# One order string, rewritten: the opening and the key, value and query stage of a transformer block

## The chip, the cores and the metric

The kernel runs on 1 core of one Trainium2 chip. The metric is device time in microseconds (us). The profile gives, beside it, a trace of one execution with the busy time of each engine: TensorE (PE, and PEld for its weight loads), VectorE (DVE), ScalarE (ACT), GpSimd (POOL) and SyncE (SP), which here issues nearly all DMAs.

## The reference

```python
# x: 2048 rows of 576, bf16; 32 heads of 18; DFF = 4608; c: one row of 576
mod = silu(c) @ w_mod                        # six rows: sa, ca, ga, sb, cb, gb
h = layernorm(x) * (1 + ca) + sa
q, k, v = split(h @ wqkv)                    # per head
pq, pk = q @ w_phi, k @ w_phi                # per head, 18 x 18
phi(p) = concat(softmax(p), softmax(-p))     # per head, 36 features
kv, z = phi(pk)^T @ v, sum_rows(phi(pk))
o = (phi(pq) @ kv) / (phi(pq) . z + 1e-6)
x = x + ga * (o @ wo)
h = layernorm(x) * (1 + cb) + sb
x = x + gb * (relu(h @ w1) @ w2)
```

## The kernel before, in words

The 2048 rows are 16 tiles of 128. Up to 90 us the kernel makes keys, values and queries for all tiles; from there on it works through the two-layer network in pairs of tiles, by loops that the change does not touch.

The first stage is a list of jobs. The string `ORDER` names them one by one, and a loop calls each (a number after a colon is the pair of PSUM banks that the job writes; pair 0 is banks 0 and 1, and so on to pair 3). Nothing is reordered afterwards: the instructions of every engine stand in its own queue in the order of the string, and an engine waits at an instruction until its data and its buffer are there. Two jobs of different engines, neither of which uses what the other writes, can therefore swap places in the string without changing any queue.

```python
    ctx.enter_context(tc.manual_schedule())
    for word in ORDER.split():
    ...
        if s:
            at[f, n] = pair(int(s))
        JOBS[f](*(() if n is None else (n,)))
```

The jobs that this document names:

- `L...` are loads by SyncE (`Lbdw` alone by ScalarE): `LwkT`, `LwqT`, `Lwv` the key, query and value weights, `Lwsc` and `Lwsh` the parts of w_mod for the scale (1 + ca) and the shift, `Lwsb` and `Lwcb` those for the second norm, `Lx...` rows of x, `Lt0` to `Lt4` blocks of x turned (features on the partitions). `wl0` to `wl4`, `w2a...` and `w2b...` load the weights of the network, `wl...` into one large buffer R1 whose start holds the early weights.
- `Z11` and `Z1` are 11 and 1 matmuls of 512 columns over zeros into bank 6, whose result nobody reads (line 238). `sc` and `sh` hold five such matmuls each, one before every five products.
- `FK` folds w_phi into the key weights: 25 small matmuls (line 450) from `LwkT` and `Lbdw`. `frd`, `fra`, `frr` copy its chunks out on VectorE and ScalarE. `FQ0` to `FQ4` (line 267) do the same for the query weights from `LwqT`, copied out by `FQrd` and `FQra`.
- `sx` (ScalarE) and `sd` (VectorE, lines 551 to 553) form silu(c). `sc` multiplies it with the scale weights on TensorE (line 259), `ca` reads the result (VectorE, line 556), `sh` does the same for the shift into the same bank, and `shc` reads that (VectorE, line 671). `m2` (line 259) and `m2c` do it for the second norm.
- `bn` are statistics of a tile on VectorE (lines 243 and 244), `sa` and `sp` the small steps on ScalarE and GpSimd that make the rows which `T` turns (TensorE, line 635) and `Tc` copies (line 638). `xd`, `xp`, `xa` multiply two tiles of turned x by the scale, on VectorE, GpSimd or ScalarE (lines 572, 565, 570).
- `KR` and `VR` (line 276) make the rows for mean and shift of the key and value weights, brought back by `KRh`, `KRd`, `VRh`, `VRd`. `QR` is the same for queries.
- `K`, `V`, `Q` are projections of a tile, 10 matmuls of 288 columns (line 282); `Ka` and `Kb` are the first 8 and the last 2 of a K. `eK` and `eQ` are their exponentials, two instructions of ScalarE (line 287); `sK` the sums on VectorE (line 292), `rK` the reciprocal by two ScalarE instructions (lines 309 and 310), `pA` and `pM` steps on GpSimd, `vE` the scaling of V on VectorE (line 313), `kv` the product of features and values (line 331).
- `sq` and `qi` send query features out and back, `qs`, `qp` and `qt` sum, scale and turn them (`qt` is a DMA that transposes, line 360). `ga`, `gb` with `gac`, `gaw`, `gar` make the two gate rows, `wo` scales the output weights by one of them. `kz`, `nu`, `ot`, `oc`, `W`, `ht` finish the first two tiles.

Of the kernel before, what the change touches and what calls it, by code (L numbers as in the profile page):

```python
# [42 lines left out]


ORDER = """
Lbdw Z11 LwkT FK Z1 fra1 Lx0 Lcc sx bn0 sd frd2 Lwsc frd0 bn1 sa0 frr sc ca Lwsh frd4 Lx2 Lid bn3 sh fra3 sp0 T0:1 shc
Lt0 KR:2 KRh0 Lwv Lx4 xd0 bn2 KRh1 mk KRd0 KRd1 Tc0 sa2 Ka0:0 VR:1 bn4 VRh0 Kb0 VRd0 sp2 VRh1 Lt1 xd2 Ka1:2 Kb1 VRd1
T2:1 eKa0 sK0 LwqT FQ3:3 Tc2 K2:0 FQra3 bn5 Lwsb eKa1 sK1 K3:3 rK0 eK2 sa4 FQ4:2 FQrd4 pM0 V0:1 sK2 Lwcb rK1 pA1 pA0
Lt2 pM1 V1:0 m2:2 eK3 FQ0:3 Lx6 vE0 V2:1 Lwga vE1 rK2 Lx10 m2c FQrd0 pA2 FQ1:3 xa4 sp4 Lt4 bn7 vE2 T4:2 Tc4 K4:0 FQra1
eK4 FQ2:2 xp6 bn6 sa6 FQrd2 sK3 Lt3 bn11 K5:1 pM2 kv0 kv1 QR:2 eK5 V3:0 kv2 QRh sp6 QRe QRd T6:2 rK3 sK4 pA3 vE3 rp  # L50
Tc6 pM3 K7:1 rK4 K6:2 pM4 pA4 eK7 eK6 Lwgb ga:0 gac V4:1 bn9 kv3 sK5 rK5 bn8 pA5 w2b0 sa8 V5:2 vE4 bn12 sp8 T8:0 xa8
pM5 vE5 Tc8 Q0:1 eQ0 gb:2 xp14 kv4 kv5 sK6 bn10 Q1:0 gbc sa10 sK7 gaw gar wl1 rK6 K8:1 qs0 wl3 bn15 eQ1 eK8 K9:2 eK9
sp10 xp10 Lwo Q2:0 pA6 sK8 pM6 eQ2 V6:1 rK8 bn13 vE6 sK9 bn14 qp0 rK7 Q3:2 pA8 T10:0 Tc10 pA7 eQ3 qs1 pM7 kv6 K10:1
eK10 rK9 K11:0 sK10 pM8 V8:2 eK11 sa14 sa12 V7:1 vE8 pM9 rK10 V9:0 vE7 xa12 sp12 pA9 kv7 T12:2 sK11 rK11 kv8 V10:1 vE9
kv9 wl0 pA10 vE10 Tc12 pM10 K12:0 sp14 T14:2 Tc14 gbw eK12 kv10 K13:1 eK13 wo2 K14:2 eK14 qt0 qs2 sK12 sK13 Q4:0 eQ4
rK13 K15:1 w2a1 qp1 V11:2 V12:0 gbr qs3 wo1 pA11 qp2 pM11 vE11 kv11 w2a2 rK12 w2a0 pA12 eK15 vE12 sK15 pM12 qt1 V13:2
kv12 pM13 Lmask sK14 Q5:1 wl4 rK15 eQ5 sq5 Q6:0 pA13 pA15 vE13 sq4 kv13 qt2 V15:2 rK14 vE15 pM15 pA14 V14:1 vE14 eQ6
Q11:2 pM14 qp3 sq6 kv14 kv15 qt3 eQ11 sq11 Q7:1 kz nu1:2 Q8:0 nu0:3 nO1 td2 eQ7 eQ8 sq7 nO0 td0 sq8 ot1:2 td1 Q9:1 oc1
Q10:0 ot0:2 wo0 wo4 eQ9 qi5 wo3 sq9 oc0 eQ10 W1:3 xr1 qi4 W0:1 lb1 Q12:2 xr0 lb0 Q13:0 lr1 eQ12 sq10 qi6 lr0 ap1 eQ13
Q14:1 ht1:2 Q15:3 ap0 wl2 ht0:0 ha eQ14 eQ15 hd w2b1 sq13 sq15 sq14 sq12  # L60
"""

SEVEN = """
# [1238 lines left out]
```

## Time and profile before

| | |
|---|---|
| median of 3 runs | 374.23 us (374.04 to 374.76) |
| the profiled execution | 374.21 us, of which the span of the trace is 372.4 us |
| TensorE busy in the span | 365.9 us (98%) |
| VectorE, ScalarE, GpSimd busy | 291.5 us (78%), 225.3 us (60%), 147.3 us (40%) |
| DMA | 50.26 MB, mean 135 GB/s |

Times in the trace count from the start of the span. Where a row ends in brackets, they hold the idle time of the engine before it and what ended it. The ends of matmuls are modelled, so the pace of TensorE is read from starts.

### The profile page before, as it was taken

To read this page: it belongs to the slowest core of one execution; us is meant where nothing else is said; L and a number is where in the kernel's file an instruction comes from. 1 tells how busy PE (TensorE), PEld (TensorE's weight loads), DVE (VectorE), ACT (ScalarE), POOL (GpSimd) and SP (SyncE) were. 2 spreads that over 40 slices of the span, in tenths; PEclk is the share of its full clock that TensorE was granted. 3 is DMA by queue.
4 is the path that set the end of the run, shared out by engine and by line. 5 is a ranking of instruction groups with operands and counts; after the bars stand their busy time and mean duration, and the time that the engine had idled before them with its cause. 6 is when DMAs were issued, how large, how long until landed. Compare 5 with 4: busy or idle time off the path is not lost.

```text
span 372.4 us, 14350 instructions
## 1 busy us (share of the span) xinstructions
PE 365.9 (98%) x6236; PEld 312.4 (84%) x6237; DVE 291.5 (78%) x540; ACT 225.3 (60%) x507; POOL 147.3 (40%) x215
## 2 busy tenths in 40 slices
PE   7999999999999999999999999999999999999996
PEld 3778788888888788889988987998799889879975
DVE  3999997679979789987897689679777857755742
ACT  2598998588632535608853874578277628835720
POOL 2167999940302567380056007402720260043023
PEclk9999999999999999999999999999999999999999
DMA  8994799787976437572164248413422304101001
GB/s 298 414 371 158 273 409 327 205 235 297 277 170 133 121 83 160 150 136 60 36 113 116 35 35 128 102 38 69 99 63 20 84 18 53 36 0 35 4 2 33
DMA packets 58880, 50.26 MB, mean 135 GB/s; under 512 B 46912, under 2 KB 51136, under 8 KB 58048
## 3 DMA queue, kind: packets, MB, share of 16 engines
q1 hardware_dynamic: 58672, 49.18, 48.9%
q8 instruction: 49, 0.80, 0.9%
q10 hardware_dynamic: 144, 0.16, 0.2%
q14 instruction: 15, 0.12, 0.1%
HBM read 32.27 MB, written 5.90 MB: 103 GB/s over the span
## 4 chain that ended last, share of the span: by engine, by line
PE 93%; DMA 4%; ACT 1%; SPq 0%; issue 0%; DVE 0%
PE PS L890 33%; PE PS L810 23%; PE PS L282 15%; PE PS L744 10%; PE PS L793 3%; DMA R<-in_wqT_dram 3%; PE PS L984 2%; PE PS L401 2%; DMA R<-in_wsc_dram 2%; PE PS L958 2%; PE PS L331 2%; PE PS L418 1%; PE PS L930 1%; ACT R L570 1%; PE PS L989 0%; PE PS L373 0%
## 5 line engine op out<-in xcount | busy, mean ns | idle before, releaser
L890 PEld LDWEIGHTS <-RH 128*128 128x128 f16 x846 | 81.5, 98 | 21.0 <-issue 0.4
L878 POOL TENSOR_TENSOR yt<-yt,gb_row 128x288 f32<-128x288 f32 x23 | 27.3, 1186 | 169.8 <-DVE yt L877 169.8
L810 PEld LDWEIGHTS <-R 64*128 64x128 bf16 (+1 forms) x1824 | 76.1, 94 | 0.7 <-issue 0.2
L890 PE MATMUL PS<-R,RH 128*128 128x288 bf16 (+1 forms) x558 | 74.5, 286 | 0.0
L810 PE MATMUL PS<-h,R 64*128 64x128 bf16 x1056 | 69.3, 216 | 0.0
L840 ACT ACTIVATE RH<-PS 128x512 f16<-128x512 f32 x96 | 50.9, 604 | 9.2 <-PE PS L810 9.1
L810 PE MATMUL PS<-RE,R 64*128 64x128 f16 x768 | 48.2, 216 | 0.0
L287 ACT ACTIVATE RT<-PS,rs 128x576 bf16<-128x576 f32 x64 | 42.9, 746 | 3.6 <-PE PS L282 3.4
L890 PE MATMUL PS<-RT,RH 128*128 128x288 f16 x288 | 38.6, 286 | 0.0
L744 PE MATMUL PS<-h,R 64*128 64x256 bf16 (+1 forms) x684 | 36.3, 264 | 0.0
L744 PEld LDWEIGHTS <-R 64*128 64x128 bf16 x684 | 31.6, 94 | 4.0 <-issue 0.2
L1047 ACT ACTIVATE h<-h,mod 128x256 bf16<-128x256 bf16 x63 | 32.8, 588 | 2.3 <-DMA h<-xn 2.3
L282 PE MATMUL PS<-RH,R 116*128 116x288 bf16 x240 | 32.5, 286 | 0.1
L810 PE MATMUL PS<-h,early 64*128 64x128 bf16 x384 | 32.0, 216 | 0.0
L282 PE MATMUL PS<-RH,RT 116*128 116x288 bf16 x240 | 31.5, 286 | 0.0
L243 DVE BATCH_NORM_STATS2 st<-x_sb 128x6 f32<-128x288 bf16 x64 | 25.8, 446 | 6.4 <-DMA x_sb<-in_xk_dram 6.3
L282 PEld LDWEIGHTS <-RT 116*128 116x128 bf16 x240 | 22.9, 98 | 5.5
L282 PEld LDWEIGHTS <-R 116*128 116x128 bf16 x240 | 22.6, 98 | 5.9 <-ACT R L638 0.4
L877 DVE TENSOR_TENSOR yt<-PS,RS 128x288 f32<-128x288 f32 x23 | 10.4, 452 | 20.6 <-PE PS L890 14.1
L810 PEld LDWEIGHTS <-w 64*128 64x128 f16 (+1 forms) x480 | 26.5, 94 | 0.0
L879 POOL TENSOR_TENSOR x_sb<-yt,x_sb 128x288 bf16<-128x288 f32 x30 | 24.9, 832 | 2.6 <-DVE yt L875 0.8
L810 PE MATMUL PS<-RE,w 64*128 64x128 f16 x384 | 25.9, 216 | 0.0
(179 smaller groups left out, 744.0 us busy)
## 6 DMA issues: line engine op xcount, KB each, us to landing
R<-in_w_dram SPq DMA_DIRECT2D x4, 1152.0 KB
eqd<-RT SPq DMA_DIRECT2D x12, 288.0 KB, 4.1
RT<-eqd SPq DMA_DIRECT2D x12, 288.0 KB, 3.0
R<-in_w2b_dram SPq DMA_DIRECT2D x2, 1296.0 KB, 6.9
R<-in_w2a_dram SPq DMA_DIRECT2D x3, 864.0 KB
out_dram<-x_sb SPq DMA_DIRECT2D x15, 144.0 KB, 1.8
x_sb<-in_xk_dram SPq DMA_DIRECT2D x10, 144.0 KB
RT<-in_xT_dram SPq DMA_DIRECT2D x2, 640.0 KB, 6.3
```

What stands on the lines that cost most here:

```text
L243: dve.bn_stats(out=s[:, hf, :], in_=x_sb[:, t % 6 if n else t, hf * HD:(hf + 1) * HD])
L282: pe.matmul(pr[:, k, 0:HD], lhsT=xt(t, ck), rhs=w[0:R, ck, k * HD:(k + 1) * HD], start=(ck == 0), stop=(ck == NC - 1))
L287: act.activation(out=E.rearrange("p (b h s e) -> p b h s e", b=2, s=2, e=DH)[:, :, :, s, :], in_=pr[:, :, 0:HD].rearrange("p b (h e) -> p ...
L744: pe.matmul(PS[:, 2 * u + hf, n * 256 + o:n * 256 + o + w], lhsT=w1_lhs(hf, c, j, h), rhs=hb[b0:b0 + 64, c, o:o + w], start=(n == 0 and c ...
L793: pe.matmul(PS[:, bank_at[n], j * 256:j * 256 + 256], lhsT=w1_lhs(hi, c, j, hi), rhs=hb[64 * hi:64 * hi + 64, c, :], start=(j == 0 and c = ...
L810: pe.matmul(PS[:, bank_at[BK[n] + str(g)], i * P:(i + 1) * P], lhsT=w[r, (4 * c + i) * P:(4 * c + i + 1) * P], rhs=x, start=(n in ("M1", " ...
L840: act.activation(out=o, in_=v[{"k11": "Y", "k12": "Z", "k21": "X", "k22": "W"}[n]], func=ACT.Relu)
L877: dve.tensor_tensor(out=y, in0=PS[:, bank, 0:HD], in1=SS[:, s, :], op=ALU.add)
L878: pool.tensor_tensor(out=y, in0=y, in1=gb_row[:, c], op=ALU.mult)
L879: eng.tensor_tensor(out=xs(t)[:, c], in0=y, in1=xs(t)[:, c], op=ALU.add)
L890: pe.matmul(PS[:, bank, 0:HD], lhsT=am[:, j, :], rhs=bm[:, j, :], start=first and j == 0, stop=(j % 9 == 8), skip_group_check=True)
L1047: act.activation(out=o, in_=o, func=ACT.Identity, scale=mod(1, c), bias=mod(0, c))
```

## The change

Only the string `ORDER` is rewritten: the same 377 jobs, in another order, some with another pair of banks. No job is added, dropped or changed.

```diff
@@ -43,21 +43,21 @@
-Lbdw Z11 LwkT FK Z1 fra1 Lx0 Lcc sx bn0 sd frd2 Lwsc frd0 bn1 sa0 frr sc ca Lwsh frd4 Lx2 Lid bn3 sh fra3 sp0 T0:1 shc
-Lt0 KR:2 KRh0 Lwv Lx4 xd0 bn2 KRh1 mk KRd0 KRd1 Tc0 sa2 Ka0:0 VR:1 bn4 VRh0 Kb0 VRd0 sp2 VRh1 Lt1 xd2 Ka1:2 Kb1 VRd1
-T2:1 eKa0 sK0 LwqT FQ3:3 Tc2 K2:0 FQra3 bn5 Lwsb eKa1 sK1 K3:3 rK0 eK2 sa4 FQ4:2 FQrd4 pM0 V0:1 sK2 Lwcb rK1 pA1 pA0
-Lt2 pM1 V1:0 m2:2 eK3 FQ0:3 Lx6 vE0 V2:1 Lwga vE1 rK2 Lx10 m2c FQrd0 pA2 FQ1:3 xa4 sp4 Lt4 bn7 vE2 T4:2 Tc4 K4:0 FQra1
-eK4 FQ2:2 xp6 bn6 sa6 FQrd2 sK3 Lt3 bn11 K5:1 pM2 kv0 kv1 QR:2 eK5 V3:0 kv2 QRh sp6 QRe QRd T6:2 rK3 sK4 pA3 vE3 rp
-Tc6 pM3 K7:1 rK4 K6:2 pM4 pA4 eK7 eK6 Lwgb ga:0 gac V4:1 bn9 kv3 sK5 rK5 bn8 pA5 w2b0 sa8 V5:2 vE4 bn12 sp8 T8:0 xa8
-pM5 vE5 Tc8 Q0:1 eQ0 gb:2 xp14 kv4 kv5 sK6 bn10 Q1:0 gbc sa10 sK7 gaw gar wl1 rK6 K8:1 qs0 wl3 bn15 eQ1 eK8 K9:2 eK9
-sp10 xp10 Lwo Q2:0 pA6 sK8 pM6 eQ2 V6:1 rK8 bn13 vE6 sK9 bn14 qp0 rK7 Q3:2 pA8 T10:0 Tc10 pA7 eQ3 qs1 pM7 kv6 K10:1
-eK10 rK9 K11:0 sK10 pM8 V8:2 eK11 sa14 sa12 V7:1 vE8 pM9 rK10 V9:0 vE7 xa12 sp12 pA9 kv7 T12:2 sK11 rK11 kv8 V10:1 vE9
-kv9 wl0 pA10 vE10 Tc12 pM10 K12:0 sp14 T14:2 Tc14 gbw eK12 kv10 K13:1 eK13 wo2 K14:2 eK14 qt0 qs2 sK12 sK13 Q4:0 eQ4
-rK13 K15:1 w2a1 qp1 V11:2 V12:0 gbr qs3 wo1 pA11 qp2 pM11 vE11 kv11 w2a2 rK12 w2a0 pA12 eK15 vE12 sK15 pM12 qt1 V13:2
-kv12 pM13 Lmask sK14 Q5:1 wl4 rK15 eQ5 sq5 Q6:0 pA13 pA15 vE13 sq4 kv13 qt2 V15:2 rK14 vE15 pM15 pA14 V14:1 vE14 eQ6
-Q11:2 pM14 qp3 sq6 kv14 kv15 qt3 eQ11 sq11 Q7:1 kz nu1:2 Q8:0 nu0:3 nO1 td2 eQ7 eQ8 sq7 nO0 td0 sq8 ot1:2 td1 Q9:1 oc1
-Q10:0 ot0:2 wo0 wo4 eQ9 qi5 wo3 sq9 oc0 eQ10 W1:3 xr1 qi4 W0:1 lb1 Q12:2 xr0 lb0 Q13:0 lr1 eQ12 sq10 qi6 lr0 ap1 eQ13
-Q14:1 ht1:2 Q15:3 ap0 wl2 ht0:0 ha eQ14 eQ15 hd w2b1 sq13 sq15 sq14 sq12
+Lbdw LwkT FK fra1 Lx0 bn0 Lcc Lwsc Lwsh Lx2 Lid Lt0 Lwv Lx4 Lt1 LwqT frd0 bn1 sx sd sa0 mk Z11 sc frd2 sp0 frd4 ca sh
+T0:0 frr bn3 Lwsb shc xd0 bn2 Z1 fra3 KR:3 Lwcb Tc0 KRh0 KRh1 KRd0 rp Lt2 Lx6 VR:2 Ka0:0 KRd1 Lt3 Kb0 sa2 xd2 VRh1
+Ka1:1 Kb1 sp2 VRh0 VRd0 T2:3 VRd1 eKa0 Lwga Tc2 eKa1 bn4 sK0 FQ3:2 FQra3 Lx10 rK0 K2:0 eK2 bn5 K3:3 pA0 eK3 FQ4:2 V0:1
+sK1 FQrd4 sK2 pM0 rK1 vE0 V1:0 pA1 vE1 sa4 rK2 m2:2 sp4 FQ0:3 pA2 FQrd0 V2:1 m2c FQ1:2 T4:3 bn6 Lt4 xa4 Tc4 K4:0 FQ2:3
+FQra1 bn7 sa6 vE2 pM2 K5:2 FQrd2 eK4 pM1 QR:1 QRh sK3 sp6 sK4 kv0 kv1 kv2 QRe QRd eK5 V3:0 xp6 sK5 T6:2 rK3 pA3 vE3
+Tc6 rK4 bn9 pM3 K7:1 pA4 rK5 K6:2 pM5 bn8 pA5 bn12 ga:0 eK7 sK7 eK6 pM4 V4:1 Lwgb gac V5:2 Q0:0 vE4 kv3 wl2 wl0 sa8
+xa8 sp8 xp14 xp10 T8:1 eQ0 kv4 vE5 kv5 Q1:2 sK6 Tc8 rK7 bn11 eQ1 gb:0 K8:1 rK6 gbc gaw bn10 bn14 K9:2 w2a0 eK8 pA6
+sa10 sK8 eK9 Q2:0 eQ2 bn15 rK8 V6:1 vE6 Q3:2 sp10 T10:0 pM7 Tc10 K10:1 Lwo pM6 qs1 bn13 eQ3 sK9 pM8 kv6 eK10 sK10
+K11:0 gar wo0 V8:2 pA8 eK11 gbw V7:1 rK9 pA7 vE7 V9:0 qp1 V10:1 vE8 pA9 sa12 sp12 vE9 sa14 sK11 T12:0 wl4 rK10 Lmask
+pA10 xa12 sp14 Tc12 K12:2 vE10 T14:0 Tc14 qs0 kv7 pM9 pM10 kv8 kv9 eK12 sK12 K13:1 rK11 qp0 qs2 eK13 rK12 sK13 w2a1
+pM11 K14:2 pM12 qt1 eK14 Q4:0 K15:1 kv10 eQ4 V11:2 gbr eK15 V12:0 w2b0 pA11 vE11 qp2 sK15 rK13 qt0 pA12 rK15 vE12 Q5:1
+wl3 pA13 sK14 pA15 Q6:2 qs3 pM13 eQ5 rK14 kv11 pA14 kv12 eQ6 pM15 sq4 V15:1 vE15 pM14 sq5 w2a2 V13:0 sq6 qp3 V14:1
+vE13 wo1 vE14 kv13 Q11:0 eQ11 kv14 kv15 Q7:2 qt2 qt3 eQ7 kz nu1:1 sq11 Q8:3 wo2 eQ8 nu0:0 nO1 w2b1 ot1:2 td2 Q9:1 oc1
+sq7 Q10:3 sq8 wo3 nO0 td1 ot0:0 eQ9 wo4 oc0 td0 W1:2 xr1 qi5 W0:1 eQ10 lb1 sq9 lr1 Q12:2 xr0 eQ12 Q13:0 sq10 lb0 lr0
+Q14:3 eQ13 qi4 ap1 ht1:2 wl1 sq12 Q15:1 ap0 ht0:0 sq13 ha hd eQ14 sq14 qi6 eQ15 sq15
```

Sorted by engine, the two strings begin so:

- TensorE before: `Z11 FK Z1 sc sh T0 KR Ka0 VR Kb0 Ka1 Kb1 T2 FQ3 K2 K3 FQ4 V0 V1 m2 FQ0 V2 FQ1 T4 K4`; after: `FK Z11 sc sh T0 Z1 KR VR Ka0 Kb0 Ka1 Kb1 T2 FQ3 K2 K3 FQ4 V0 V1 m2 FQ0 V2 FQ1 T4 K4`.
- VectorE before: `bn0 sd frd2 frd0 bn1 frr ca frd4 bn3 shc xd0 bn2`; after: `bn0 frd0 bn1 sd frd2 frd4 ca frr bn3 shc xd0 bn2`.
- SyncE, both: `LwkT Lx0 Lcc Lwsc Lwsh Lx2 Lid Lt0 Lwv Lx4 Lt1 LwqT Lwsb Lwcb Lt2 Lx6`; then before `Lwga Lx10 m2c Lt4 Lt3 QRd Lwgb`, after `Lt3 Lwga Lx10 m2c Lt4 QRd Lwgb`.

## The prediction

> **What bounds the kernel now.** I first cut the span into stretches and asked each for the busy time of the engines (columns: stretch and length, then busy time and instructions of PE, PEld, DVE, ACT, POOL, then granted clock, DMA share, GB/s).
>
> ```profile
> 1.29:5.59 4.30, 4.29 (x11) 1.41 (x11) 0.00 (x0) 0.71 (x1) 1.13 (x4) 1.00 0.87 282
> 5.59:7.13 1.54, 1.42 (x27) 1.43 (x27) 0.81 (x2) 0.64 (x2) 0.00 (x0) 1.00 1.05 428
> 12.41:17.91 5.50, 5.22 (x43) 4.53 (x43) 5.30 (x19) 3.86 (x10) 0.62 (x3) 1.00 1.02 413
> 17.91:27.92 10.01, 9.88 (x135) 8.03 (x135) 9.85 (x17) 9.49 (x28) 6.18 (x13) 1.00 0.95 375
> 27.92:90.21 62.29, 62.29 (x695) 50.90 (x697) 53.94 (x89) 52.49 (x123) 46.30 (x87) 1.00 0.80 265
> 90.21:372.40 282.19, 278.66 (x5270) 243.68 (x5270) 216.64 (x398) 156.41 (x341) 91.53 (x99) 1.00 0.39 84
> ```
>
> From 27.92 to 90.21 TensorE has work in all of 62.29 us, and from 12.41 to 27.92 it misses 0.28 and 0.13. What it does there is the same after the change, in another order. So no order can win more than these 0.4 us behind 12.41, and TensorE passes a late start at 12.41 on to the end almost whole. Only what lies ahead of 12.41 can move the time much. That is where the timeline comes in, and there the job that changes its place is `Z11`, eleven matmuls whose result nobody reads: first in TensorE's queue before, now behind `FK` and ahead of `sc`.
>
> ```profile
> 1.30 4.38 PE L238 MATMUL PS<-early 128*128 128x512 bf16 x11 [1.30 <-POOL eps_t L230]
> 2.55 0.15 PEld L238 LDWEIGHTS <-early 128*128 128x128 bf16 x1 [0.28 <-issue]
> 2.98 0.15 PEld L238 LDWEIGHTS <-early 128*128 128x128 bf16 x1 [0.28 <-issue]
> 4.69 0.15 PEld L238 LDWEIGHTS <-early 128*128 128x128 bf16 x1 [0.28 <-issue]
> 5.09 0.10 PEld L238 LDWEIGHTS <-early 128*128 128x128 bf16 x1 [0.25 <-issue]
> 5.59 1.54 PEld L450 LDWEIGHTS <-R 126*128 126x128 bf16 x25 [0.41 <-DMA R<-in_wkT_dram]
> 5.80 1.49 PE L450 MATMUL PS<-RS,R 126*128 126x126 bf16 x25
> 7.13 0.60 PE L238 MATMUL PS<-early 128*128 128x512 bf16 x2
> 8.20 0.28 PE L259 MATMUL PS<-siluc,R 116*128 116x1 bf16 x5 [0.48 <-DMA R<-in_wsc_dram]
> 12.01 0.27 PE L635 MATMUL PS<-ident,early 128*128 128x128 bf16 x2
> 12.42 1.43 PE L276 MATMUL PS<-RH,RS 116*100 116x288 bf16 x10
> 17.91 0.45 PE L267 MATMUL PS<-RS,R 126*128 126x126 bf16 x6 [0.28 <-DMA R<-in_wqT_dram]
> ```
>
> The reader is to see three things. `Z11` now runs while TensorE waits for the key weights anyway (they let `FK` go at 5.59): it costs nothing. `FK` is done when `Z1` starts at 7.13, and `sc` starts at 8.20, set by the landing of its weights. And the starts of the weight loads show the pace: 0.43 us for 512 columns from 2.55 to 4.69, then faster. In the chain of waits a group of 20 matmuls of 288 columns takes 2.45 us, which is 0.425 ns a column or 0.218 us for 512:
>
> ```profile
> 18.35 2.45 PE PS L282 x20
> ```
>
> So the first matmuls ran at half pace, until about 5.05, or 3.75 us after the first. The granted clock reads 1.00 in that stretch too; I go by the starts. That the pace comes with a while of work, rather than at a fixed time, is my reading; this trace has one start only.
>
> **The change part by part.** *`Z11` behind `FK`.* Nothing is ahead of `FK` now, so it starts at the same 5.80 (its load is first on SyncE in both orders), but at half pace. At full pace its 25 matmuls took 7.13 - 5.80 = 1.33 us; times 0.43 / 0.218 = 1.97 that is 2.6, so it ends at 8.4. Then come the eleven. If the half pace lasts 3.75 us from 5.80 as it did from 1.30, it ends at 9.55: until then 1.15 / 0.43 = 2.7 matmuls, and the other 8.3 at 0.218 take 1.8. `sc` can start at 11.35 instead of 8.20: 3.15 us late.
>
> [...]
>
> The bounds from rows: at full pace throughout, `FK` ends at 7.13 and the eleven at 7.13 + 11 x 0.218 = 9.53. Then silu(c) is later, since `sd` is moved behind `frd0` and `bn1` on VectorE:
>
> ```profile
> 6.32 0.82 DVE L243 BATCH_NORM_STATS2 st<-x_sb 128x6 f32<-128x288 bf16 x2 [6.32 <-DMA x_sb<-in_xk_dram]
> 7.17 0.21 DVE L244 BATCH_NORM_AGGREGATE mv<-st 128x2 f32<-128x12 f32 x1
> 7.30 0.12 DVE L551 TENSOR_SCALAR sg<-sg 116x5 f32<-116x5 f32 x1
> 7.67 0.17 DVE L553 TENSOR_TENSOR siluc<-ccol,sg 116x5 bf16<-116x5 bf16 x1
> 7.75 1.26 DVE L459 CAST RH<-PS 116x504 bf16<-116x504 f32 x2
> ```
>
> The statistics end at 7.38, one copy takes 0.63, the second statistics 1.06, the three silu steps 0.54: 9.6. That is the earliest start of `sc`, 1.4 us late, and at 11.35 it hides behind the eleven. At half pace throughout, `sc` starts at 8.4 + 11 x 0.43 = 13.1, 4.9 us late. I take 3.15, since the one start in this trace lasted 3.75 us.
>
> *From `sc` to `KR`.* The steps are the same, with the same waits (`sh` for `ca`, `KR` for `shc`): 12.42 - 8.20 = 4.2 us. `Z1` now stands between `T0` and `KR`, in a gap from about 12.12 (two transposes of 128 columns at 0.425 ns from 12.01) to 12.42; its 0.22 fit, and cost 0.2 if that cover went. VectorE has `frr` and `bn3`, about 1.5 us, ahead of `shc`, but `shc` waits for `sh`, about 1.8 us behind `ca`. So `KR` starts about 15.55.
>
> *The loads.* SyncE's queue has the same first sixteen loads in the same order, and nothing that it is moved past makes it wait. So, whatever the words of the change say, shift, value and query weights and the first turned blocks come no earlier than before: cost and gain nothing. Only `Lt3` goes four places up.
>
> *From `KR` to 27.92.* The query weights let `FQ3` go at 17.91 after a wait of 0.28 that the late start covers. Against that VectorE and ScalarE were busy for 9.85 and 9.49 of 10.01 us, with the same work behind `KR` in both orders, so they give TensorE little room: `FQ3` now writes the banks of `VR` and has to wait for `VRd1`. I count a gain of 0.15, between 0 and 0.4.
>
> *From 27.92 to 90.21.* No wait can go, so a new order can only add some. Two places look tight, both where `rK` is moved up on ScalarE (`rK5` ahead of `eK7`, `rK7` ahead of `eQ1`):
>
> ```profile
> 34.04 2.64 ACT L287 ACTIVATE RT<-PS,rs 128x576 bf16<-128x576 f32 x4
> 36.72 0.28 ACT L309 ACTIVATE early<-early 128x64 f32<-128x64 f32 x1
> 37.03 0.26 ACT L310 ACTIVATE early<-early 128x64 f32<-128x64 f32 x1
> 35.56 1.40 PE L282 MATMUL PS<-RH,R 116*128 116x288 bf16 x10
> 42.76 5.15 ACT L287 ACTIVATE RT<-PS,rs 128x576 bf16<-128x576 f32 x8
> ```
>
> `eK7`, the first half of the four at 34.04, ended about 35.36, and `V4` overwrites its banks from 35.56: 0.2 us of slack. The reciprocal takes 0.57 (36.72 to the next start at 37.29), so `V4` would wait about 0.35. Queued behind `rK5` are `eK7` and `eK6`. `rK7` pushes a block of eight exponentials, back to back in 5.15 us, by the same 0.57; part of it reaches `Q3`, which waits for `eK9` to leave its banks. I take 0.4 for both, between 0 (the slack is elsewhere) and 1.1 (both whole).
>
> *Near 75 us* `w2a2` (864 KB) now goes out just ahead of the transposes `qt2` and `qt3`, whose landing lets `eQ8` and `eQ9` write.
>
> ```profile
> 71.97 1.31 SPq L360 DMA_TRANSPOSE RE<-RT  x1
> DMA to landing us min/median/max: 3.6/6.7/9.7
> 78.49 1.38 ACT L287 ACTIVATE RT<-PS,rs 128x576 bf16<-128x576 f32 x2 [0.23 <-PE PS L282]
> 79.76 0.70 ACT L695 ACTIVATE oT<-PS 128x640 bf16<-128x640 bf16 x1
> 81.68 2.61 PE L418 MATMUL PS<-wo_sb,oT 128*128 128x288 bf16 x20
> ```
>
> Issued at 71.97 and landing after the median 6.7 it would come at 78.7 against `eQ8` at 78.49; behind it `oc1` ended 80.46, and `W1` began at 81.68. So 1.2 us are covered: nothing. At the longest landing, 9.7, `eQ8` would wait until 81.7, and 2.0 us would show. The late loads (`wl1` last instead of `wl2`, `w2b1` earlier) meet no wait, since nothing between 90 and 360 shows TensorE idle; nothing.
>
> *Sum*, against the profiled execution's own 374.21 (the median of the runs is 374.23, the span 372.4): 3.15 - 0.15 + 0.4 = 3.4, so 377.6.
>
> **The rivals.** *Full pace from the start.* The early half pace belongs to the first microseconds of a program, not to idleness. Then silu(c) sets `sc`: 1.4 - 0.15 + 0.4 = 1.65, so 375.9. For it: the granted clock of 1.00. Against it: that reads 1.00 where the starts show half.
>
> *Half pace through all eleven.* The half pace lasts longer this time than in the one start that I have: 4.9 - 0.15 + 0.4 = 5.15, so 379.4. For it: if what ends it is work done, `FK` starts it with shorter matmuls than the eleven were; and the runs of before can't show how much its length varies, since there a late change of pace is covered by the wait to 8.20. Against it: 3.75 us is the only length seen.
>
> *The late start is absorbed.* The loads, not TensorE, set the pace up to 17.91 (`FQ3` waits for query weights), so a late `KR` is made up. It decides if the start slips by less than that wait and the 0.13 behind it, 0.4 in all; then the rest is covered and the time is 374.2, not slower. It needs `sc` by 8.6. Against it: even at full pace the eleven end at 9.53.
>
> **How the numbers follow.** The forecast of 377.6 has 0.70, full pace 0.08, half pace throughout 0.12, absorbed 0.04; 0.06 is for something that I don't see, half of it on either side. The forecast's own range is 376.8 to 378.8: a half pace of 3.4 to 5 us, and waits behind `KR` between -0.4 and 1.1. The range from 376.2 to 379.8 adds the half pace throughout and part of what lies between; the case of full pace and the absorbed one stay outside. 0.2% is 0.75 us, about what the runs of this kernel can tell from no change. Slower by more: forecast, both paces and half of the unseen, 0.93. Within: the absorbed one, 0.04. Faster: the other half of the unseen, 0.03.
>
> **What would show it.** In the timeline after: TensorE empty until 5.8; `FK` taking about 2.6 us; weight loads of line 238 first 0.43 and then 0.22 apart; the first matmul of line 259 at 11 to 12 with no wait for a DMA; line 276 at 15 to 16; no wait of line 267 for the query weights; and at 90.2 + 3.4 = 93.6 the first line 744. The forecast is wrong if `FK` keeps its 1.33 us, if line 276 starts before 14 or after 17, or if the start of line 744 is shifted by 1 us more or less than line 276.

## The result and the profile after

The changed kernel took 378.49 us (median, 378.08 to 378.65) against 374.44 us (374.04 to 374.76) for the kernel before on the same chip: a ratio of 1.0107, 95% interval 1.0089 to 1.0125. The profiled execution took 378.65 us with a span of 376.9; the one before, 374.21 and 372.4. So the two traces differ by 4.5 us, and that is what has to be found.

First the same kind of cut as before, at the changed kernel's own marks (same columns: busy time and instructions of PE, PEld, DVE, ACT, POOL, granted clock, DMA share, GB/s).

```profile
1.29:5.59 4.30, 0.10 (x2) 0.21 (x3) 0.00 (x0) 0.71 (x1) 1.14 (x4) 1.00 0.85 285
5.49:11.06 5.57, 5.57 (x37) 3.69 (x37) 4.08 (x12) 1.76 (x6) 0.00 (x1) 1.00 1.01 389
14.87:19.93 5.06, 5.06 (x44) 4.54 (x44) 4.90 (x18) 3.41 (x10) 0.62 (x3) 1.00 1.01 416
30.00:93.91 63.91, 63.09 (x692) 50.77 (x694) 54.75 (x89) 52.85 (x122) 47.43 (x84) 1.00 0.87 265
93.91:376.70 282.79, 278.79 (x5272) 243.76 (x5270) 216.73 (x398) 156.67 (x341) 91.53 (x99) 1.00 0.36 80
```

TensorE is empty up to 5.49, then shows hardly a gap until 19.93. New is the row from 30.00 to 93.91: TensorE misses 0.82 us there, where it missed nothing in the stage before. The timeline of the changed kernel gives the marks (the second column is the length of a group; a row ends in the idle time before it and what ended that):

```profile
5.49 2.56 PE L450 MATMUL PS<-RS,R 126*128 126x126 bf16 x25 [5.49 <-DMA RS<-in_bdw_dram]
7.85 3.37 PE L238 MATMUL PS<-early 128*128 128x512 bf16 x12
8.27 0.15 PEld L238 LDWEIGHTS <-early 128*128 128x128 bf16 x1 [0.28 <-issue]
8.69 0.15 PEld L238 LDWEIGHTS <-early 128*128 128x128 bf16 x1 [0.27 <-issue]
9.12 1.61 PEld L238 LDWEIGHTS <-early 128*128 128x128 bf16 x8 [0.28 <-issue]
11.06 0.27 PE L259 MATMUL PS<-siluc,R 116*128 116x1 bf16 x5
12.74 0.16 DVE L556 TENSOR_SCALAR ca<-PS 116x5 f32<-116x5 f32 x1 [2.43 <-PE PS L259]
14.87 2.65 PE L276 MATMUL PS<-RH,RS 116*100 116x288 bf16 x20
19.93 0.44 PE L267 MATMUL PS<-RS,R 126*128 126x126 bf16 x6
86.67 1.40 PE L418 MATMUL PS<-wo_sb,oT 128*128 128x288 bf16 x10 [0.28 <-ACT oT L695]
93.91 2.29 PE L744 MATMUL PS<-h,R 64*128 64x128 bf16 x73
96.66 2.13 PE L744 MATMUL PS<-h,R 64*128 64x256 bf16 x35 [0.46 <-DMA R<-in_w_dram]
```

`FK` runs at half pace: from its start to the first of the eleven it takes 2.36 us (5.49 to 7.85) instead of 1.33. Weight loads of line 238 start 0.42 and 0.43 apart until 9.12, then eight within 1.61 us, 0.2 each: the half pace ends there. Beside the marks of before, one of which is not shown yet:

```profile
10.50 0.26 PE L259 MATMUL PS<-siluc,R 116*128 116x1 bf16 x5 [0.41 <-DVE ca L556]
90.14 4.15 PE L744 MATMUL PS<-h,R 64*128 64x128 bf16 x108
```

| first start of | before | after | later by | forecast |
|---|---|---|---|---|
| `FK` (line 450) | 5.80 | 5.49 | -0.31 | 0 |
| `sc` (line 259) | 8.20 | 11.06 | 2.86 | 3.15 |
| `KR` (line 276) | 12.42 | 14.87 | 2.45 | 3.15 |
| `FQ3` (line 267) | 17.91 | 19.93 | 2.02 | |
| line 744 | 90.14 | 93.91 | 3.77 | 3.4 |
| end of the span | 372.4 | 376.9 | 4.5 | 3.4 |

Up to `FQ3` the change costs 2.0 us. From `FQ3` to line 744 it costs another 1.75 (73.98 against 72.23) and behind line 744 another 0.73. The waits of TensorE in the changed kernel explain only part of this:

```profile
PE PS L450 <- DMA RS<-in_bdw_dram: 5.5, 1, 5.5
PE PS L744 <- DMA R<-in_w_dram: 0.5, 1, 0.5
PE PS L635 <- DVE RT L313: 0.3, 1, 0.3
PE PS L418 <- ACT oT L695: 0.3, 1, 0.3
```

A matmul group is longer in the timeline than its share of the chain: 10 of line 282 show 1.40 us in the prediction's timeline, where their share in its chain is 1.23. A gap of up to 0.17 us can therefore show as busy there, and many small ones can add up unseen. The chain of the changed kernel says what they wait for. Before, it was TensorE from 27.92 to 90.21; now it leaves TensorE in that stretch, for GpSimd and above all for four transfers:

```profile
39.30 7.77 DMA gatd<-gt
47.14 7.06 DMA ga_row<-gatd
78.31 6.23 DMA RE<-RT
88.77 7.84 DMA R<-in_w_dram
```

And the queues of SyncE, GpSimd and ScalarE at those places:

```profile
72.82 0.43 SPq L606 DMA_DIRECT2D R<-in_w2a_dram  x1
74.86 6.11 SPq L360 DMA_TRANSPOSE RE<-RT  x2
88.77 0.46 SPq L614 DMA_DIRECT2D R<-in_w_dram  x1
54.34 1.28 POOL L690 TENSOR_TENSOR wo_sb<-wo_sb,ga_row 128x576 bf16<-128x576 bf16 x1 [1.30 <-DMA ga_row<-gatd]
56.33 1.42 DVE L313 TENSOR_TENSOR RT<-PS,early 128x576 bf16<-128x576 f32 x2 [0.82 <-POOL early L652]
82.07 1.38 ACT L287 ACTIVATE RT<-PS,rs 128x576 bf16<-128x576 f32 x2 [0.70 <-DMA RE<-RT]
84.64 1.38 ACT L287 ACTIVATE RT<-PS,rs 128x576 bf16<-128x576 f32 x2 [0.61 <-DMA RE<-RT]
```

Three places, each a job that the string moved. **`wo0`** stands ahead of `pA8` and `pA7` now: GpSimd waits 1.30 us in it for the gate row, `pA` comes late, VectorE's scaling of V waits 0.82 (the row at 56.33) and then 0.38 for GpSimd, and TensorE 0.33 for VectorE (line 635 in its waits). **`w2a2`** goes out at 72.82, ahead of `qt2` and `qt3`. Their row of 6.11 us holds 3.05 and 2.66 us for the two and 0.40 between them, in which the second waited for its data from GpSimd; before, the two took 1.31 and 1.29. `eQ8` and `eQ9` wait 0.70 and 0.61 for them. **`wl1`** goes out last, at 88.77, and line 744 waits 0.46 for it at 96.66.

### The profile page after: what moved, and what is told of

Same layout as the page of the kernel before. It is cut to its first block, busy times and chain, and to the rows that moved or that the text cites. A ratio compares the mean times of both kernels' runs of the same rounds, so it can differ in the third digit from the quotient of the medians.

```text
span 376.9 us, 14356 instructions
## 1 busy us (share of the span) xinstructions
PE 366.3 (97%) x6237; PEld 313.3 (83%) x6237; DVE 292.3 (78%) x540; ACT 225.7 (60%) x507; POOL 148.1 (39%) x215
## 4 chain that ended last, share of the span: by engine, by line
PE 83%; DMA 9%; POOL 4%; ACT 2%; issue 1%; DVE 1%; SPq 0%; ACTq 0%; DVEq 0%; POOLq 0%
PE PS L890 32%; PE PS L810 23%; PE PS L744 9%; PE PS L282 5%; PE PS L793 3%; DMA R<-in_w_dram 2%; DMA gatd<-gt 2%; DMA ga_row<-gatd 2%; POOL RT L299 2%; PE PS L984 2%; DMA RE<-RT 2%; PE PS L958 2%; PE PS L238 1%; PE PS L401 1%; DMA RS<-in_bdw_dram 1%; ACT RT L287 1%
```

## The experiments

In the diffs `-` and `+` are moves in the order string. "276 to 744" is the time from the first line 276 to the first line 744 in the profile, "744 to end" from there to the end of the span; they show a delay behind the opening whatever the opening did. Each is read from one execution: the changed kernel itself took 79.04 and 80.15 us from 276 to 744 in its two. Ratios are to the kernel before on the same chip, with 95% intervals.

| kernel | first 276 | 276 to 744 | 744 to end | median us | ratio |
|---|---|---|---|---|---|
| before | 12.42 | 77.72 | 282.26 | 374.44 | |
| changed | 14.87 | 79.04 | 282.99 | 378.49 | 1.0107 (1.0089 to 1.0125) |
| changed, again | 15.79 | 80.15 | 282.26 | 378.84 | 1.0122 (1.0099 to 1.0146) |
| changed, `Z11` first | 14.14 | 80.30 | 282.66 | 377.36 | 1.0071 (1.0045 to 1.0097) |
| before, `Z11` behind `FK` | 16.42 | 77.72 | 282.16 | 377.88 | 1.0083 (1.0069 to 1.0096) |
| changed, no `Z11` | 13.00 | 78.62 | 283.78 | 377.56 | 1.0081 (1.0055 to 1.0106) |
| before, no `Z11` | 13.46 | 77.72 | 282.12 | 374.95 | 1.0007 (0.9998 to 1.0016) |
| changed, `wl1` early | 15.57 | 78.45 | 282.18 | 377.67 | 1.0088 (1.0064 to 1.0111) |
| changed, `w2a2` early | 15.11 | 78.11 | 283.28 | 379.36 | 1.0136 (1.0111 to 1.0160) |
| changed, `wo0` late | 16.18 | 78.56 | 283.96 | 379.40 | 1.0131 (1.0110 to 1.0151) |
| changed, all three moves | 16.06 | 78.55 | 282.19 | 378.05 | 1.0091 (1.0069 to 1.0113) |
| changed, opening back | 13.15 | 79.04 | 282.01 | 376.57 | 1.0063 (1.0040 to 1.0085) |
| opening and three places back | 13.02 | 77.81 | 282.47 | 374.53 | 1.0011 (0.9998 to 1.0024) |
| the same, `ca` first | 12.41 | 78.27 | 282.52 | 374.64 | 1.0002 (0.9989 to 1.0015) |

**The place of the eleven matmuls.** In the kernel before, `Z11` alone is put behind `FK`:

```diff
-Lbdw Z11 LwkT FK Z1 fra1
+Lbdw LwkT FK Z11 Z1 fra1
```

> The kernel before with Z11 alone moved behind FK. Theory: FK at half pace to about 7.9, the eleven to 10.9, Z1 to 11.1, sc 2.9 us late, less 0.4 for the wait for query weights that goes: 376.9 us, with no wait on a DMA behind 20 us. Rival (absorbed): 374.4. Rival (the opening is the whole change): 378.5.

It cost 0.83% by itself: 377.88 us, where 376.9 was expected. Its timeline:

```profile
8.10 4.67 PE L238 MATMUL PS<-early 128*128 128x512 bf16 x13
11.08 0.15 PEld L238 LDWEIGHTS <-early 128*128 128x128 bf16 x1 [0.28 <-issue]
11.51 0.77 PEld L238 LDWEIGHTS <-early 128*128 128x128 bf16 x4 [0.28 <-issue]
12.61 0.27 PE L259 MATMUL PS<-siluc,R 116*128 116x1 bf16 x5
16.42 1.43 PE L276 MATMUL PS<-RH,RS 116*100 116x288 bf16 x10
```

`FK` takes the same 2.36 us (5.74 to 8.10), but the half pace lasted to about 11.5 in this execution, 5.8 us, which the expectation did not have, and line 276 starts 4.0 late. From there to line 744 it takes 77.72 us, exactly as before, and so does the rest to 0.1: the delay of the opening is passed on whole, and nothing is added. So the forecast's main mechanism is shown on its own, and what the changed kernel loses behind the opening comes from other moves.

The other way round, in the changed kernel `Z11` alone goes back to the head:

```diff
-Lbdw LwkT FK ... sa0 mk Z11 sc frd2
+Lbdw Z11 LwkT FK ... sa0 mk sc frd2
```

> The changed kernel with Z11 alone moved back to the head of TensorE's queue. Theory (the change costs 2.0 to 2.5 us at the opening, where Z11 stands in the way of sc, and another 2 us later, where three loads come late): sc then waits for silu(c), ready at 9.13 in the changed kernel, so it starts at about 9.25 instead of 11.06, KR moves from 14.87 to about 13.1 and everything behind it by the same 1.8: about 376.7 us, with the three later waits still there. Rival (all of the loss comes from the opening, the later waits only follow from it): 374.4 us, no later waits. Rival (the opening's loss is absorbed by the loads anyway): 378.5.

It took 377.36 us, where 376.7 was expected. By the medians it got back only about a third of the loss, and its interval overlaps that of the changed kernel. The profile is of an execution of 378.86 us, 1.5 above the median. In it `sc` now waits for silu(c), the second part of the changed opening, as the forecast's rival of full pace had it (it put `sc` at 9.6, the trace says 9.30):

```profile
9.30 0.26 PE L259 MATMUL PS<-siluc,R 116*128 116x1 bf16 x5 [1.89 <-DVE siluc L553]
```

Yet line 276 starts at 14.14, 4.84 us behind `sc` instead of 4.22. Cut into microseconds, the granted clock of this execution shows why (the last but two column):

```profile
10.00:11.00 1.00, 0.92 (x18) 0.66 (x18) 0.45 (x2) 0.00 (x0) 0.00 (x0) 1.00 1.08 403
11.00:12.00 1.00, 0.98 (x13) 0.51 (x12) 0.89 (x4) 0.00 (x0) 0.91 (x5) 0.68 1.04 429
12.00:13.00 1.00, 1.00 (x14) 0.47 (x12) 0.79 (x3) 0.00 (x0) 0.07 (x1) 0.50 0.96 392
14.00:15.00 1.00, 1.00 (x6) 0.91 (x6) 1.00 (x6) 0.05 (x1) 0.00 (x0) 0.61 1.09 448
15.00:16.00 1.00, 1.00 (x10) 1.00 (x9) 0.93 (x4) 0.79 (x3) 0.09 (x1) 1.00 0.97 406
```

After the gap of 1.89 us the clock fell back to a half from about 11.4 to 14.8 (by the means of these slices). That is in this one trace; in all the others the granted clock is 1.00 from 8 to 16 us.

**Without the eleven.** Both kernels, `Z11` taken out (its result is read by nobody):

```diff
-... sa0 mk Z11 sc frd2          (changed)
+... sa0 mk sc frd2
-Lbdw Z11 LwkT FK Z1             (before)
+Lbdw LwkT FK Z1
```

> The changed kernel with Z11 left out (eleven matmuls whose result nobody reads). Theory: Z11 costs only its own length there; FK at half pace ends at 7.85, sc starts with silu(c) at 9.25 and the pace is full by about 9.2, so the time is that of e1, 376.7 (up to 377.0). Rival (the eleven are needed to get the pace up): sc and sh hold ten more matmuls of 512 columns and run at half pace, up to 2.1 us later: 378.5 or more, with weight loads of line 238 apart by 0.43 plus the products.

> The kernel before with Z11 left out. Theory: FK at half pace ends about 7.9, Z1 takes 0.43, sc starts at 8.3 and is slow until about 9.2: KR is 0.5 us late, of which the wait for the query weights covers 0.3 to 0.4: 374.6 us (374.4 to 374.9). Rival (short products do not bring the pace up): 375.5 or more.

In the kernel before the eleven are worth 0.07% (-0.02% to 0.16%): at most little. Its 374.95 us lie just above the range that was expected; line 276 started 1.04 late in its profile instead of 0.5, since the first matmuls ran at half pace for longer than was thought, to beyond 10 us (line 238 starts 0.56 us apart at 8.97, 9.53 and 10.09, 0.35 at 12.01 and 12.36). In the changed kernel, expected at 376.7, taking them out does as much as putting them first, as far as the times tell; the two intervals lie on each other. But there the saved time leaks: line 276 starts at 13.00, 0.58 behind the kernel before, and 744 to end grows to 283.78, since line 744 now waits 1.88 us for `wl1`:

```profile
95.79 2.13 PE L744 MATMUL PS<-h,R 64*128 64x256 bf16 x35 [1.88 <-DMA R<-in_w_dram]
```

**The three places one by one.** `wl1` behind `wl4`, or `w2a2` behind `w2a1`, or `wo0` behind `pA15`, in the changed kernel:

```diff
-ap1 ht1:2 wl1 sq12       +T12:0 wl4 wl1 rK10
-vE15 pM14 sq5 w2a2 V13:0 +sK13 w2a1 w2a2 pM11
-K11:0 gar wo0 V8:2       +sK14 pA15 wo0 Q6:2
```

> The changed kernel with one load moved: wl1 right behind wl4 on SyncE (issued about 49 us) instead of behind qi4 (88.77 us). Theory: in the changed kernel the second step of the network waited for it until 96.66, some 0.6 us; that wait goes: about 377.8 us, no wait of line 744 for a DMA. Rival (the wait was covered by something just as late, activations or banks): 378.5.

> The changed kernel with w2a2 moved behind w2a1 on SyncE, out of the place just ahead of qt2 and qt3. Theory: the transposes then start on an empty queue and land by 80 us, eQ8 and eQ9 wait for nothing, oc0 is in time and W0 does not wait: 0.6 to 0.7 us less, about 377.8 us. Rival (the transposes are slow because they are two in a row behind sq6, not because of w2a2): 378.5, both transposes still taking 3 us each to issue.

> The changed kernel with wo0 moved behind pA15 on GpSimd. Theory: wo0 held GpSimd 1.3 us waiting for the gate row and 1.28 us for itself, pA8 and pA7 came late, VectorE waited 0.82 and TensorE stood at T12 for about 0.5 us; all that goes: 377.7 to 378.0 us. Rival (T12 waits since V7, V9 and V10 now stand in a row and VectorE can't clear their banks in time): 378.5, the wait of line 635 still there.

> The changed kernel with all three of these moves (wl1 behind wl4, w2a2 behind w2a1, wo0 behind pA15), opening as in the changed kernel. Theory: 2.0 us less than the changed kernel, 376.5 us, what is left being the opening. Rival (the waits share a cause, or each makes place for another): 377.5 to 378.5.

None of the four medians can be told from the changed kernel, since all the intervals overlap. Only `wl1` came near what was expected (377.67 against 377.8); `w2a2` and `wo0` missed it by 1.5 us or so, and all three together took 378.05 instead of 376.5, as the rival had it. The profiles tell more. TensorE's wait went when its job moved: with `wl1` early, no line 744 waits for a DMA and 744 to end is 282.18; with `w2a2` early, the two transposes take 1.31 and 1.30 us to issue, `eQ8` waits for TensorE and no longer for a transpose, and 276 to 744 is 78.11; with `wo0` late, line 635 no longer waits, though VectorE still waits 0.77 for GpSimd at the first of its two waits there, as it does in every kernel below with `wo0` moved. So that wait is not the work of `wo0`. But then the next wait in the row grew. The first of these rows is ScalarE's timeline with `w2a2` early, the second the waits of that kernel, the last two the waits with `wo0` late.

```profile
81.57 1.37 ACT L287 ACTIVATE RT<-PS,rs 128x576 bf16<-128x576 f32 x2 [0.23 <-PE PS L282]
PE PS L744 <- DMA R<-in_w_dram: 1.0, 1, 1.0
```

```profile
PE PS L744 <- DMA R<-in_w_dram: 1.3, 1, 1.3
PE PS L418 <- POOL wo_sb L690: 0.4, 1, 0.4
```

The wait for `wl1` grew from 0.46 to 1.0 and 1.3. Line 744 did not come earlier for it (5.41 and 5.32 us behind the issue of `wl1`, 5.14 in the changed kernel); the transfer took longer, 8.62 and 8.88 us instead of 7.84. Why it did is not shown. And behind `pA15` `wo0` was too late: `W1` waited 0.4 for it, in this kernel and in the one with all three moves, where the second transpose also went out late, at 80.1, and an exponential waited 0.54 for it. That one is a flawed test of `wo0` for this reason, and it leaves 0.83 of the 1.32 us between line 276 and line 744 in place.

**The opening, then the places, on one chip.** First the opening alone goes back (`Z11` first, silu(c) ahead of `frd0` and `bn1`), then also the three jobs, `wo0` this time behind `pA13`; the changed kernel itself ran beside them.

```diff
-Lbdw LwkT FK fra1 Lx0 bn0 Lcc Lwsc ... frd0 bn1 sx sd sa0 mk Z11 sc
+Lbdw Z11 LwkT FK fra1 Lx0 bn0 Lcc sx sd Lwsc ... frd0 bn1 sa0 mk sc
```

> The changed kernel with the opening of the kernel before: Z11 at the head of TensorE's queue, and sx and sd behind Lcc, ahead of frd0 and bn1. Theory: KR starts at 12.4 as before, the wait for the query weights returns, and what is left are the waits behind: T10 to nu 0.4 to 0.8, transposes up to 0.7, wl1 0.5 to 1.9 (it grows when TensorE comes earlier): 376.0 us, between 375.6 and 376.8, runs within 1 us of each other. Rival (all of the loss is the opening): 374.5.

> The same opening, and the three later places mended as well: wl1 behind wl4, w2a2 behind w2a1, wo0 behind pA13 on GpSimd (where it was idle 1.4 us). Theory: nothing of size is left but the short waits behind ScalarE near 38 and 60 us: 374.5 to 375.0 us, within 0.2% of the kernel before. Rival (the new order of keys, values and queries costs by itself): 375.5 or more.

> The changed kernel once more, unaltered, on the chip of the next two. [...] Rival (the half pace always lasts the same): all within 0.6 us of 378.5, as in the first four runs.

From 378.84 the opening takes 2.27 us off, the three places another 2.04, to 374.53; 0.41 is left to the kernel before, at 374.12 on that chip, which the interval does not tell from nothing. The three intervals (1.0099 to 1.0146, 1.0040 to 1.0085, 0.9998 to 1.0024) don't touch. By the medians of the spans alone the two steps are 2.45 and 1.8. So the loss is shown to be in two parts of about the same size, undone in this order. The profiles, one execution each, show the first step at line 276, from 15.79 to 13.15, and less of the second: line 276 stays (13.02), 276 to 744 goes from 79.04 to 77.81, against 77.72 before, but the rest grows by 0.46.

The changed kernel's six runs spread from 377.91 to 380.70, over 2.8 us; the rival's "within 0.6 us of 378.5" was wrong. With the opening back the median came as expected, but line 276 at 13.15 and not at 12.4, without a wait for the query weights, and the runs spread over 3.1 us instead of 1 (their spans over 2.1).

What is left of the opening, 0.60 us at line 276, is in the waits of TensorE with all back, and in the timelines of TensorE and VectorE:

```profile
PE PS L259 <- DVE ca L556: 0.8, 1, 0.8
5.96 1.80 PE L450 MATMUL PS<-RS,R 126*128 126x126 bf16 x25
7.69 0.17 DVE L551 TENSOR_SCALAR sg<-sg 116x5 f32<-116x5 f32 x1 [0.42 <-ACT sg L667]
8.20 0.68 DVE L459 CAST RH<-PS 116x504 bf16<-116x504 f32 x1
9.76 1.22 DVE L459 CAST RH<-PS 116x504 bf16<-116x504 f32 x2
10.90 0.15 DVE L556 TENSOR_SCALAR ca<-PS 116x5 f32<-116x5 f32 x1
```

`ca` runs at 10.90 instead of 10.30, behind two copies of `FK`. The last kernel gives it its old place:

```diff
-sc frd2 sp0 frd4 ca sh T0:0 frr bn3
+sc frd2 frr sp0 ca frd4 sh T0:0 bn3
```

> The changed kernel with the opening of the kernel before (eleven matmuls first, sx and sd on their old places) and wl1, w2a2 and wo0 on their old places, and on VectorE the order of the kernel before around ca: frr behind frd2, frd4 behind ca. Theory: the 0.65 us by which the first line 276 still stood late in the run without this edit came from ca standing behind frd2 and frd4 on VectorE (ca ran at 10.90 there, line 259 waited 0.8 us for it). With ca first again line 276 starts at about 12.4, part of the wait for the query weights returns, and the time is 374.0 to 374.4 us, within 0.2% of the kernel before. Rival: what is left of the new order costs by itself, elsewhere; then the time stays at 374.5 us or above, though line 276 starts earlier.

Its waits:

```profile
PE PS L259 <- DVE ca L556: 0.5, 1, 0.5
PE PS L267 <- DMA R<-in_wqT_dram: 0.5, 1, 0.5
```

Line 276 starts at 12.41, as before, the wait for the query weights is back; but the place of `ca` is the smaller part of this. With all back the half pace lasted into `FK`, although `Z11` came first: from the start of `FK` to the next matmul it took 1.65 us (5.96 to 7.61) instead of 1.33. Its first chunk was copied late on ScalarE, so `sx` behind it was late, VectorE waited 0.42 for that in `sd`, and its first copy of `FK` began at 8.20 instead of 7.75. From there to `ca` it took 2.70 us; in the last kernel and in the kernel before, 2.55. So the order gives 0.15 of the 0.60, and 0.45 is the longer half pace of that execution, which the last kernel's execution did not have (`FK` in 1.33 us, 5.83 to 7.16). The ratio is 1.0002 (0.9989 to 1.0015): within 0.2%, as was expected, though at 374.64 us, since the kernel before stood at 374.62 on this chip. The step from the run ahead of it is not shown by the times, whose intervals overlap, only by the profile; there 0.46 of the 0.61 us is given back behind line 276 (78.27 against 77.81). No kernel was faster than the one before.

## Why the prediction was right, and where not

**The direction and the main mechanism were right.** Nothing hid the half pace once `FK` came first. `sc` was forecast 5.55 us behind the start of `FK` (5.80 to 11.35); it came 5.57 behind it (5.49 to 11.06). That the two agree so well is luck. `FK` up to the next matmul was forecast at 2.6 and took 2.36, 1.77 times its 1.33 and not 1.97 times; and between `FK` and line 259 stand twelve matmuls of 512 columns, not eleven, since `sc` begins with one of its own (x12 in the row at 7.85). The two errors, 0.26 and 0.22, nearly cancel. And in the other five profiles with this opening the same step took 5.62 to 6.56. The waits for scale and query weights went, the late start was passed on, and "absorbed" fell with it.

**The opening was 0.7 us dearer in the forecast than in the trace.** Of these, 0.31 is `FK`, whose data landed earlier in this execution (other runs of the changed opening began it between 5.66 and 5.94). The other 0.41 is a step that failed: "The steps are the same, with the same waits" from `sc` to `KR`. The kernel before waited 0.41 in there for `ca`; with `sc` late VectorE had been idle for 2.43 us when `ca` came, the wait no longer shows, and it took 3.81. That wait for VectorE shrank with `sc` 2.86 later (from the matmul ahead of it to line 259 it is 0.39 us, 12.57 to 12.96, instead of 0.78, 9.72 to 10.50); I had carried it over as if it were work.

**Behind `KR`** I counted a gain of 0.15 up to 27.92, between 0 and 0.4. To `FQ3` it was 0.43 (5.49 to 5.06), the full wait for the query weights and the gaps beside it; 0.05 of it was lost again by `FQ2`, the line 267 that begins at 28.17 before and at 30.24 after. So 0.38 was gained, near the upper bound.

**The length of the half pace was the right thing to doubt.** I sized it from one start, 3.75 us; the changed kernel had 3.6. But the same string had line 276 at 15.79 in its other profiled run, and the six profiles with this opening spread from 14.87 to 16.18; up to 0.45 of this is the start of `FK` (5.49 to 5.94). No run shows the 3.4 us of half pace with which the forecast's own range begins: in these six profiles it lasted 3.6 to 5.7 us by the starts of the weight loads. The rival "half pace through all eleven" (`sc` 4.9 late) is nearly what the kernel before with `Z11` behind `FK` did in its profile (4.4 late).

**Three steps costed at nothing were wrong, and together as dear as the opening.** (1) "So 1.2 us are covered: nothing" for `w2a2` ahead of the transposes. I took the landing from the issue times of before. But behind `w2a2` the two transposes took 3.05 and 2.66 us to issue instead of 1.31 and 1.29, and both exponentials waited, not one. The row with the longest landing, which would have shown 2.0, was nearer: the exponentials waited 1.3 us in all here, and 2.6 in the other profile of the same kernel. (2) "The late loads ... meet no wait, since nothing between 90 and 360 shows TensorE idle." In the kernel before `wl1` went out with `wl3` at 42.67, and the load that went out last, at 87.00, was `wl2`:

```profile
42.67 1.20 SPq L614 DMA_DIRECT2D R<-in_w_dram  x2
87.00 0.41 SPq L614 DMA_DIRECT2D R<-in_w_dram  x1
```

That no reader of `wl2` waited there says nothing of `wl1` going out at 88.77. The question was its landing time against the start of line 744, and that was not worked out. (3) `wo0` ahead of `pA8` was not looked at. It puts a wait for a DMA (1.30 us in the changed kernel) in GpSimd's queue in front of work that VectorE needs. By the runs on one chip the three are worth 2.04 us (their forecast was 0); in the profile of the changed kernel 0.75 of it appears from `T10` to `nu`, 0.68 from `nu` to line 744 and about 0.5 behind it. The 0.4 for the `rK` moves was too much: from `T4` to `T10`, where both lie, the delay grew by 0.25.

The forecast's own test failed: line 744 was shifted by 1.3 us more than line 276 (3.77 against 2.45), where over 1 was to count as wrong. The time still came out within 1 us, because the opening was put too high by about as much as part of what was missed. So the opening carried the forecast, and that the sum came so near is in part luck.

**How sure this is.** Shown by runs: the cost of `Z11` behind `FK` alone, the cost of the opening as a whole, and that of the three places together. Only read from profiles: the share of each place. Over all the profiles of kernels with the new order these shares are (seven profiles with the job in its changed place, except where said):

| stretch | before | job in the changed place | job moved |
|---|---|---|---|
| `T10` to `nu` (`wo0`) | 28.39 | 28.81 to 29.14 | 28.52 twice behind `pA13`, 28.79 and 28.80 behind `pA15` |
| `nu` to 744 (`w2a2`) | 13.45 | 13.46 to 15.38 | 13.45 to 13.46 in three, 14.00 where `wo0` was too late |
| 744 to end (`wl1`) | 282.26 | 282.01 to 283.96 | 282.18 to 282.52 in four |

So `wo0` cost 0.3 to 0.6 us, and 0.13 of the new order stays there; `w2a2` and `wl1` cost anything from nothing to nearly 2 us, and mostly not both: where the second stretch was short with `wl1` last (13.46 twice), the third was 283.28 and 283.78, where it was long (15.38 and 15.14), 282.26 and 282.66. Not settled: why a place costs so differently in different executions, and how much of the spread of the times is the half pace.

## What to carry to other kernels

When a job is moved, price its DMA too: its landing time in the new order against the first reader, and what stands behind any instruction that waits for it; an idle-free stage in the old order is no cover (`wl1`, issued at 88.77, made line 744 wait 0.46 us in such a stage). Don't carry a wait over as if it were work when its start moves: here the one for `ca` shrank by 0.4 us with `sc` 2.86 later, and with `Z11` first `sc` waited 1.89 us for silu(c), for which it had not waited in the changed kernel. And when several moved jobs each cause a wait along the same path, undo them together: here, with the wait at `w2a2` or at `wo0` gone, the one for `wl1` was longer in the profile (1.0 and 1.3 us instead of 0.46), and the times showed no gain.

## What the hardware showed that I had not expected

The half pace at the start had no fixed length. By the starts of the weight loads it lasted from the first matmul 3.6 us (5.49 to 9.1) in the changed kernel and 5.8 (5.74 to 11.5) with `Z11` behind `FK`, for the same instructions in the same order up to there. With `Z11` first it ended at about 5.05 before, but reached into `FK`, beyond 5.96, in two kernels with the opening back (`FK` in 1.65 and 1.87 us instead of 1.33). The granted clock read 1.00 all the same: before from 1.29 to 5.59, in the changed kernel from 5.49 to 11.06, with `Z11` behind `FK` from 8 to 12. What sets the length is not shown.

The clock also fell back to a half from 11.4 to 14.8, 3.4 us, in the changed kernel with `Z11` first. Ahead of it stood a gap of 1.89 us, and TensorE was busy for 0.41 us from 7 to 9 and for 0.70 from 9 to 10. That is one trace, and what brought it on is not shown.

A small DMA behind bulk loads was slow: the first transfer of the gate row (1.1 KB) took 7.77 us behind `wl2` and `wl0`, the second (144 KB) 7.06, and the row was ready only 15 us after its issue (39.30 to 54.2). In the kernel before, with `w2b0` in front, the second transfer went out 5.42 us behind the first (36.88 and 42.30) instead of 7.84, and took 4.1 us. No run moves these loads alone, so that they are the cause is not shown.
